# Splitting the modulation row of an adaLN block: scale first, values from unshifted rows, the shift added to the kv matrix afterwards

## The chip, the cores and the metric

The kernel runs on one core of one Trainium2 chip. The metric is the device time of one execution in microseconds (us), and the figure quoted for a kernel is the median of its fast runs unless something else is said. A profile is one execution seen by the hardware profiler; its span is about 2 us shorter than the device time of that execution. PE is the matmul engine, DVE the vector engine, ACT the scalar engine, POOL the GpSimd engine; SP issues most loads. "L764" is a line of the kernel. The line numbers differ between kernels, so the text says what each line does.

## The reference, cut to what matters

```python
mod = (silu(c) @ w_mod).reshape(1, 6, 1, -1)
sa, ca, ga, sb, cb, gb = (mod[:, i] for i in range(6))   # shift, scale, gate; twice
h = layernorm(x) * (1 + ca) + sa
q, k, v = split(h @ wqkv)                                # 2048 tokens, 32 heads of 32
pq, pk = phi(q), phi(k)                                  # elu + 1
kv = einsum('bhsd,bhse->bhde', pk, v);  z = pk.sum(tokens)
x = x + ga * ((pq @ kv) / (pq . z)) @ wo
h = layernorm(x) * (1 + cb) + sb
x = x + gb * (gelu(h @ w_gate) * (h @ w_up)) @ w_down    # the longest part of the time
```

Tokens are handled in four blocks of 512. A block has four x tiles of 128 tokens.

## The kernel before

A small planner records every operation, then orders each engine's instructions with a list scheduler that uses a model of costs. PE's order is the program's; the order on DVE, ACT, POOL and SP is the planner's. So one edit can move operations far away.

The opening loads two x tiles, then all 4 MB of the first modulation weights (`ModSet(0)` makes the shift row and the scale row together), then two more x tiles:

```python
def start_phase():
    xs = [load_x(0), load_x(1)]
    ms0 = ModSet(0, wm0_ring, psM)          # 8 loads of 512 KB: shift and scale
    xs += [load_x(2), load_x(3)]
    load_w(Wk[:, :, 0:NW], D, NW)
    ...
    xh = [ln_rows(x) for x in xs[0:2]]      # layernorm of rows on DVE
    transpose_h(halves[0], 0, xh[0]); keep_warm(3, NW)
    transpose_h(halves[0], 1, xh[1]); keep_warm(2, NW)
    for kt in range(KD):                    # row sums, with idle filler matmuls between
        ms0.step(); keep_warm(2, NW)
    ms0.columns(...)                        # row -> per-partition columns
    evac_h(0, halves[0])                    # h = xhat * scale + shift, from PSUM
    return [ln_rows(x) for x in xs[2:4]], halves[1]
```

`evac_h` evicts half of block 0: four operations on DVE, four on ACT. The second half follows after two key groups. Keys of block 0 come next (8 groups of 8 matmuls), then its values by a Strassen scheme (7 products, 56 matmuls), whose combinations, sums and copies run on DVE and ACT:

```python
blocks = [k0 + V[0]]                        # block 0: keys, then values
...
def comb(ps, sb, i, row, col):              # DVE, reads PSUM
    tt_op(dst(i, row, col), v3(ps), v3(sb), ALU.add)
```

Blocks 1 to 3 are normalized from x, written to memory, read back by a transposing load, and then scaled and shifted on DVE:

```python
def ln1_block(b):
    for tl in range(TT):
        xt = load_x(b * TT + tl)
        mv = ln_stats(xt)                   # DVE statistics
        rstd = pool_rstd(mv)                # POOL
        ve.scalar_tensor_tensor(out=nb, in0=mv[:, 0:1], scalar=-1.0, in1=rstd, ...)
        ac.activation(out=xh, in_=xt, func=AF.Identity, scale=rstd, bias=nb)
        gp.dma_start(out=xa_scr[b][...], in_=xh)
    sy.dma_start_transpose(out=hr1[b], in_=xa_scr[b][:])
    for kd in range(KD):
        ve.tensor_scalar(out=hr1[b][:, kd, :], ..., op0=ALU.mult, op1=ALU.add)
```

## Time and profile before

| | before |
|---|---|
| median of the first 5 runs | 778.31 us (777.8 to 781.81) |
| span of the profile | 776.5 us |
| PE busy | 754.3 us, 97% |
| first key matmul | 21.03 us |
| block 1's first key matmul | 54.48 us |
| block 2's first kv product | 85.68 us |

The page's first part gives the busy time of each engine, its share of the span and its number of instructions:

```profile
span 776.5 us, 10117 instructions
PE 754.3 (97%) x3656; PEld 345.3 (44%) x3680; DVE 553.2 (71%) x1091; ACT 376.7 (49%) x655; POOL 67.7 (9%) x142
```

PE is the bound of the whole, but a busy PE is not a useful PE. The timeline of PE (start, duration, engine, line, operation, shapes, count, and in brackets the idle time before it with what ended it) shows the opening. L489 makes row sums, L542 is filler, L764 keys, L557 transposes, L702 values:

```profile
16.65 0.40 PE L489 MATMUL psum<-mem 128*32 128x512 bf16 x4 [0.34 <-DMA mem<-in_w_mod_dram]
...
21.03 3.61 PE L764 MATMUL psum<-mem 128*128 128x512 bf16 x15 [2.04 <-DMA mem<-in_A_wqkv_dram]
24.48 1.06 PE L557 MATMUL psum<-mem 128*128 128x128 f16 x16
29.34 12.45 PE L764 MATMUL psum<-mem 128*128 128x512 bf16 x47 [3.80 <-DVE mem L549]
...
54.48 3.62 PE L764 MATMUL psum<-mem 128*128 128x512 bf16 x16
```

PE waits for the last modulation weights until 16.65 us, starts useful work at 21.03 us, and stands still for 3.80 us before 29.34 us. Then 47 matmuls take 12.45 us. Windows of 2 us (bounds, length, busy time of each engine with its count, then granted clock, DMA share and GB/s) show why they are slow, and three longer windows show DVE's load in the first 14 us, from there to block 1, and through block 1:

```profile
30.00:32.00 2.00, 2.00 (x6) 0.65 (x6) 1.90 (x5) 1.24 (x1) 1.15 (x3) 0.52 1.05 380
32.00:34.00 2.00, 2.00 (x7) 0.80 (x6) 1.97 (x7) 1.28 (x3) 0.21 (x1) 0.62 0.95 371
0.00:14.00 14.00, 7.52 (x51) 3.36 (x52) 5.15 (x22) 2.38 (x6) 2.64 (x20) 1.00 0.83 315
14.00:54.48 40.48, 33.27 (x165) 14.31 (x165) 34.63 (x86) 25.47 (x43) 10.66 (x21) 0.96 0.73 246
54.48:85.68 31.20, 31.04 (x167) 15.12 (x168) 22.55 (x58) 16.80 (x29) 5.06 (x9) 1.00 0.49 155
```

The clock was 0.52 and 0.62 of full speed after the standstill. DVE (the third busy time) worked 34.63 us of the 40.48 us between 14 us and block 1, but only 22.55 us of 31.20 in block 1.

### The profile page before, as it was taken

To read this page: it belongs to the slowest core of one execution; us is meant where nothing else is said; L and a number is where in the kernel's file an instruction comes from. 1 tells how busy PE (TensorE), PEld (TensorE's weight loads), DVE (VectorE), ACT (ScalarE), POOL (GpSimd) and SP (SyncE) were. 2 spreads that over 40 slices of the span, in tenths; PEclk is the share of its full clock that TensorE was granted. 3 is DMA by queue.
4 is the path that set the end of the run, shared out by engine and by line. 5 is a ranking of instruction groups with operands and counts; after the bars stand their busy time and mean duration, and the time that the engine had idled before them with its cause. 6 is when DMAs were issued, how large, how long until landed. Compare 5 with 4: busy or idle time off the path is not lost.

```text
span 776.5 us, 10117 instructions
## 1 busy us (share of the span) xinstructions
PE 754.3 (97%) x3656; PEld 345.3 (44%) x3680; DVE 553.2 (71%) x1091; ACT 376.7 (49%) x655; POOL 67.7 (9%) x142
## 2 busy tenths in 40 slices
PE   6799999999989999999999999999999999999997
PEld 2344545444434444444444444444444444444444
DVE  3895976479997877899878462776777767646254
ACT  1765656569779477775544202315455444430000
POOL 1230300000021212221000000010000000000000
PEclk9999999999999999999999999999999999999999
DMA  8837130591279747767566557852332323355441
GB/s 331 305 109 230 60 51 1 195 330 60 68 221 277 234 156 240 230 201 230 166 214 228 193 217 210 251 163 56 107 95 69 109 60 103 117 196 198 168 158 46
DMA packets 130178, 129.12 MB, mean 166 GB/s; under 512 B 32720, under 2 KB 109136, under 8 KB 129104
## 3 DMA queue, kind: packets, MB, share of 16 engines
q1 hardware_dynamic: 121600, 105.40, 43.7%
q0 software_dynamic: 6176, 20.98, 7.3%
q10 hardware_dynamic: 2352, 2.10, 0.8%
q8 instruction: 29, 0.48, 0.2%
q14 instruction: 21, 0.17, 0.1%
HBM read 98.04 MB, written 23.07 MB: 156 GB/s over the span
## 4 chain that ended last, share of the span: by engine, by line
PE 84%; DVE 6%; DMA 4%; ACT 3%; issue 1%; SPq 1%; POOL 0%; DVEq 0%; POOLq 0%; ACTq 0%
PE psum L1038 39%; PE psum L1143 22%; PE psum L764 7%; PE psum L702 5%; PE psum L945 5%; PE psum L730 4%; DVE mem L472 4%; DMA mem<-in_A_x_dram 1%; DVE mem L514 1%; DMA mem<-in_B_w_up_dram 1%; DMA mem<-in_w_mod_dram 1%; PE psum L775 1%; DMA mem<-in_B_w_down_dram 1%; DVE mem L800 1%; SPq L481 1%
## 5 line engine op out<-in xcount | busy, mean ns | idle before, releaser
L1038 PE MATMUL psum<-mem 128*128 128x512 f16 x1568 | 339.2, 379 | 0.3 <-ACT mem L633 0.2
L472 DVE TENSOR_TENSOR mem<-psum,mem 128x512 f16<-128x512 f32 (+3 forms) x302 | 202.1, 681 | 117.4 <-PE psum L1143 39.3
L1038 PEld LDWEIGHTS <-mem 128*128 128x128 f16 (+1 forms) x1568 | 153.4, 98 | 185.8 <-issue 1.1
L472 DVE TENSOR_TENSOR mem<-mem 128x1024 f16<-128x1024 bf16 (+9 forms) x415 | 211.5, 538 | 30.0 <-DMA mem<-in_B_w_up_dram 7.7
L633 ACT ACTIVATE mem<-psum 128x512 f32<-128x512 f32 x232 | 135.7, 594 | 178.2 <-PE psum L1038 89.2
L1143 PE MATMUL psum<-mem 128*128 128x512 f16 (+2 forms) x789 | 169.1, 375 | 0.5
L1143 PEld LDWEIGHTS <-mem 128*128 128x128 f16 x798 | 78.1, 98 | 91.4
L1051 ACT ACTIVATE mem<-mem 128x512 f16<-128x512 f16 x84 | 52.8, 629 | 77.7 <-DVE mem L472 77.7
L764 PE MATMUL psum<-mem 128*128 128x512 bf16 x244 | 59.5, 387 | 6.4 <-DVE mem L549 3.8
L945 PE MATMUL psum<-mem 128*128 128x512 f16 x256 | 57.9, 379 | 0.1
L730 PE MATMUL psum<-mem 128*128 128x512 f16 x224 | 51.2, 379 | 0.0
L702 PE MATMUL psum<-mem 128*128 128x512 f16 (+1 forms) x223 | 50.6, 379 | 0.7 <-ACT mem L633 0.6
L764 PEld LDWEIGHTS <-mem 128*128 128x128 f16 x256 | 25.2, 99 | 37.0 <-DVE mem L549 5.4
L945 PEld LDWEIGHTS <-mem 128*128 128x128 bf16 x256 | 24.8, 98 | 32.4 <-DVE mem L472 3.0
L621 ACT ACTIVATE mem<-psum 128x512 f16<-128x512 f32 x40 | 23.6, 594 | 27.8 <-PE psum L764 22.9
L730 PEld LDWEIGHTS <-mem 128*128 128x128 f16 (+1 forms) x224 | 21.4, 98 | 26.5 <-issue 2.1
L514 DVE BATCH_NORM_STATS2 mem<-mem 128x6 f32<-128x512 bf16 x48 | 31.7, 681 | 2.1 <-DMA mem<-in_A_x_dram 1.8
L702 PEld LDWEIGHTS <-mem 128*128 128x128 f16 x224 | 21.6, 98 | 25.8 <-issue 0.9
L626 DVE TENSOR_SCALAR mem<-mem 128x512 f16<-128x512 f16 x56 | 15.7, 284 | 15.7 <-ACT mem L621 15.5
L924 ACT ACTIVATE mem<-mem 128x512 f16<-128x512 f16 x28 | 20.3, 799 | 10.6 <-DMA mem<-xhs 10.6
L623 ACT ACTIVATE mem<-psum 128x512 f16<-128x512 f32 x40 | 23.7, 595 | 0.0
L788 ACT ACTIVATE mem<-psum,mem 128x512 f32<-128x512 f32 x32 | 21.4, 679 | 4.3 <-PE psum L786 3.3
(97 smaller groups left out, 383.0 us busy)
## 6 DMA issues: line engine op xcount, KB each, us to landing
mem<-in_B_w_gate_dram SPq DMA_DIRECT2D x28, 512.0 KB, 4.1
mem<-in_B_w_up_dram SPq DMA_DIRECT2D x28, 512.0 KB, 5.3
mem<-ts SPq DMA_DIRECT2D x8, 1792.0 KB, 6.9
mem<-in_w_mod_dram SPq DMA_DIRECT2D x24, 512.0 KB, 6.5
mem<-in_B_w_down_dram SPq DMA_DIRECT2D x6, 1792.0 KB, 7.5
mem<-in_A_x_dram SPq DMA_DIRECT2D x32, 256.0 KB, 3.9
mem<-in_B_w_down_dram SPq DMA_DIRECT2D x14, 512.0 KB, 6.0
ts<-mem POOLq DMA_DIRECT2D x14, 512.0 KB, 3.5
```

Source lines behind the costliest of these rows:

```text
L472: ve.tensor_tensor(out=out, in0=a, in1=b, op=op)
L514: ve.bn_stats(out=stats[:, cb, :], in_=xt[:, cb * BW:(cb + 1) * BW])
L621: ac.activation(out=e, in_=t, func=AF.Exp)
L623: ac.activation(out=r, in_=t, func=AF.Relu)
L633: ac.activation(out=t, in_=ps, func=AF.Copy)
L702: te.matmul(ps, lhsT=A[:, k, i * P:(i + 1) * P], rhs=B[:, k, :], start=(start and k == 0), stop=(k == KH - 1), skip_group_check=True)
L730: te.matmul(o, lhsT=W[:, k, (j0 + i) * P:(j0 + i + 1) * P], rhs=h_form(a, k), start=(start and k == 0), stop=(k == KH - 1), skip_group_che ...
L764: te.matmul(ps, lhsT=hr1[b][:, k, tl * P:(tl + 1) * P], rhs=Wk[:, k, n * NW:(n + 1) * NW], start=(k == 0), stop=(k == KD - 1))
L945: te.matmul(psw, lhsT=pqT[b][:, g, tl * P:(tl + 1) * P], rhs=Wp[:, g, cs], start=(g == 0), stop=(g == KD - 1))
L1038: te.matmul(ps, lhsT=a[:, u, k, :], rhs=b[:, k, :], start=(start and k == 0), stop=(k == KH - 1), skip_group_check=True)
L1051: ac.activation(out=t, in_=src, func=AF.Gelu_apprx_tanh)
L1143: te.matmul(ps, lhsT=a[:, i, q * P:(q + 1) * P], rhs=b[:, i, :], start=(start and i == 0), stop=(i == NPR - 1), skip_group_check=True)
```

## The change

The intent is to start useful matmuls with half of the modulation weights. Write block 0's rows as h = s + sa, where s = xhat * (1 + ca) needs only the scale. Then v = s Wv + sa Wv, and the kv matrix of the block is pk' (s Wv) + z (sa Wv). So the kernel can make block 0's values from s, and add z times one row, sa Wv, to the kv matrix later. Keys pass through a nonlinear phi and still need the full h. The core of the diff, with cuts:

```diff
 def start_phase():
-    xs = [load_x(0), load_x(1)]
-    ms0 = ModSet(0, wm0_ring, psM)
-    xs += [load_x(2), load_x(3)]
+    for tt in range(TT): xs.append(load_x(tt)); loads.append(plan.ops[-1])
+    ca = ModRow(1, wm_ca, {4: loads[2], 6: loads[3]})      # scale: 2 MB
+    load_w(Wv...)                                          # value weights, in three parts
+    sa = ModRow(0, wm_sa)                                  # shift: 2 MB
     load_w(Wk[:, :, 0:NW], D, NW)
 ...
+    for i in range(KH):
+        ca.step(i)
+        if i >= 0 and i < 2: tile_of(2 + i)                # transposes of tiles 2 and 3
+        keep_warm(2, NW)
+    ca.columns(opcA, 1.0, lambda: keep_warm(2, NW))
+    for f in scale: f()                                    # 32 small evictions: s = xhat * scale
+    for n, tl in ((0,0),(0,1),(0,2),(0,3),(1,0),(1,1)): v_plain(tl, n)   # 8 matmuls each
+    for i in range(KH): sa.step(i)
+    sa.columns(modT[:, 0:KD], 0.0, lambda: v_plain(2, 1))
+    v_plain(3, 1)
+    for kd in range(KD):                                   # h = s + shift, for the keys
+        ve.tensor_scalar_add(out=hr1[0][:, kd, :], in0=hs0[:, kd, :], scalar1=modT[:, kd:kd + 1])
+
+def shift_row():                                           # 16 narrow row sums: sa Wv
+    ...
+    def add(ch):                                           # during block 1
+        te.matmul(psr, lhsT=selr[:, ch, :], rhs=row, start=True, stop=True)
+        for g in range(4):                                 # kv += z * (sa Wv)
+            ve.scalar_tensor_tensor(out=o, in0=psr[...], scalar=kvzacc[:, 4*ch+g, P:P+1], in1=o, ...)
 ...
-blocks = [k0 + V[0]]
+blocks = [k0]                                              # block 0: only keys are left here
-    put(0, 2 + i, F(h_sum, 0, j), WV(j, 0), WV(j, 1))
-    put(1, i, F(h_sum, 1, j))
+    put(0, 3 + j, WV(j, 0), WV(j, 1))
+    put(1, i, F(h_sum, 0, j), F(h_sum, 1, j))              # block 0's sums move into block 1
 ...
+plan.moves = [(mods[1], kfin[3]), ([rows[3, 3]], relu)]    # two corrections to the planner's order
```

Left out above: the list of block 0 is now shorter, and the normalizing of blocks 1 and 2 is put at its steps 0 and 4 instead of 2 and 8.

The new `moves` take operations out of the planner's order and put them behind another operation. The first brings forward the scaling of block 1's rows on DVE. The second puts off the last normalized row of block 3 on ACT.

More of the change, by code (lines that the diff above doesn't have):

```diff
@@ L234, in order, with moved @@
         return [self.ops[n] for _, n in best[1]]
+    moves, drops, extra = (), (), ()
+    def moved(self):
+        ops = self.order()
+        for group, after in self.moves:
+            ops = [o for o in ops if o not in group]
+            i = ops.index(after) + 1
+            at = {o: j for j, o in enumerate(ops)}
+            late = [self.ops[p] for o in group for p in o.preds if self.ops[p] not in group and at[self.ops[p]] >= i]
+            assert not late, [(l.eng, l.line, at[l] - i) for l in late]
+            ops[i:i] = group
+        for group, before in self.extra:
+            i = ops.index(before)
+            ops[i:i] = group
+        return [o for o in ops if o not in self.drops]
     def issue(self):
         with self.tc.manual_schedule():
-            for op in self.order():
+            for op in self.moved():
                 if op.line not in self.calls:
@@ L326, with __init__ @@
     class Banks:
-        def __init__(self, lo, hi):
-            self.lo, self.n, self.i = lo, hi - lo + 1, 0
+        def __init__(self, lo, hi, skip=0):
+            self.lo, self.n, self.i = lo, hi - lo + 1, skip
         def __call__(self, dt=FP32):
@@ L352 @@
         nc.gpsimd.memset(selb[DH * j:DH * j + 1, j, :], 1.0)
+    sel2 = at(3.25, [2], F16)
+    nc.vector.memset(sel2, 0.0)
+    selr = at(164, [2, P], F16)
+    nc.gpsimd.memset(selr, 0.0)
+    for j in range(4):
+        nc.vector.memset(sel2[DH * j:DH * j + 1, j % 2:j % 2 + 1], 1.0)
+        nc.gpsimd.memset(selr[DH * j:DH * j + 1, j % 2, :], 1.0)
+    sarep = at(164.5, [KD, DH], F16)
     eps5 = at(1.75, [1], FP32)
@@ L378 @@
     vta = Ring(51.75, [KD, P + 2], F16, 4).slots
-    wm0_ring = Ring(60, [MW], BF16, 7)
-    wm0_ring.slots += Ring(176, [MW], BF16, 1).slots
+    wm_ca, wm_sa = at(60, [KD, D], BF16), at(176, [KD, D], BF16)
+    hs0 = at(152, [KD, TG], F16)
     Wq = at(60, [KD, D], BF16)
@@ L440 @@
     psK0, psK = Banks(4, 7), Banks(4, 5)
-    psD = Banks(5, 5)
+    psD, psV0, psR = Banks(5, 5), Banks(0, 5, 4), Banks(7, 7)
     QA, QB = Banks(0, 1), Banks(2, 3)
@@ L466, in load_x, with load_w @@
         return xt
-    def load_w(dst, col, n=D):
-        sy.dma_start(out=dst, in_=A_wqkv[:, col:col + n].rearrange("(kd p) n -> p kd n", p=P))
+    def load_w(dst, col, n=D, k0=0, k1=KD):
+        sy.dma_start(out=dst, in_=A_wqkv[k0 * P:k1 * P, col:col + n].rearrange("(kd p) n -> p kd n", p=P))
     def tt_op(out, a, b, op):
@@ L509, in spread, with __init__, step, columns @@
                 ac.activation(out=dst[:, h * NW:(h + 1) * NW], in_=psr, func=AF.Copy, scale=scale)
+    class ModRow:
+        def __init__(self, m, wm, before={}):
+            self.wm, self.ps = wm, None
+            for i in range(0, KD, 2):
+                sy.dma_start(out=wm[:, i:i + 2, :],
+                             in_=w_mod[i * P:(i + 2) * P, m * D:(m + 1) * D].rearrange("(k p) n -> p k n", p=P))
+                if i in before:
+                    plan.aim(before[i])
+        def step(self, i):
+            if i == 0:
+                self.ps = psM()
+            row_sums(self.ps, srep, self.wm, i)
+        def columns(self, dst, add, between=None):
+            row = mrow_ring()
+            ve.tensor_copy(out=row, in_=self.ps)
+            if between is not None:
+                between()
+            psc = psM()[:, 0:KD].rearrange("p (j c) -> p j c", c=2)
+            for jj in range(4):
+                te.matmul(psc[:, jj, :], lhsT=row[:, jj * P:(jj + 1) * P], rhs=sel2,
+                          start=True, stop=True, skip_group_check=True)
+            ve.tensor_scalar_add(out=dst.rearrange("p (c j) -> p c j", j=4), in0=psc.rearrange("p j c -> p c j"),
+                                 scalar1=add)
+    def row_sums(ps, rep, W, i):
+        for p in range(2):
+            for ch in range(2):
+                o = DH * (2 * p + ch)
+                te.matmul(ps[o:o + DH, :], lhsT=rep[:, 2 * i + p, :], rhs=W[:, 2 * i + p, ch * NW:(ch + 1) * NW],
+                          start=(i == 0), stop=(i == KH - 1))
     def ln_stats(xt):
@@ L543, in keep_warm, with start_tile, scale, v_plain @@
                              start=True, stop=True, skip_group_check=True)
-    def evac_h(h, pss):
-        for kd in range(KD):
-            src, dst = pss[kd // 4][:, kd % 4, :], hr1[0][:, kd, h * HB:(h + 1) * HB]
-            if kd < KD // 2:
-                ve.tensor_scalar(out=dst, in0=src, scalar1=opcA[:, kd:kd + 1], scalar2=modT[:, kd:kd + 1],
-                                        op0=ALU.mult, op1=ALU.add)
-            else:
-                ac.activation(out=dst, in_=src, func=AF.Identity, scale=opcA[:, kd:kd + 1],
-                                     bias=modT[:, kd:kd + 1])
-    def transpose_h(pss, tl, xh):
+    def start_tile(pss, tl, xh):
         for kd in range(KD):
             te.transpose(pss[kd // 4][:, kd % 4, (tl % 2) * P:(tl % 2 + 1) * P], xh[:, kd * P:(kd + 1) * P],
-                                ident)
-    def start_phase():
-        xs = [load_x(0), load_x(1)]
-        ms0 = ModSet(0, wm0_ring, psM)
-        xs += [load_x(2), load_x(3)]
+                         ident)
+        def scale():
+            for kd in range(KD):
+                src, dst = pss[kd // 4][:, kd % 4, (tl % 2) * P:(tl % 2 + 1) * P], hs0[:, kd, tl * P:(tl + 1) * P]
+                if kd < KH:
+                    ve.tensor_scalar_mul(out=dst, in0=src, scalar1=opcA[:, kd:kd + 1])
+                else:
+                    ac.activation(out=dst, in_=src, func=AF.Copy, scale=opcA[:, kd:kd + 1])
+        return scale
+    def v_plain(tl, n):
+        ps = psV0()
+        for k in range(KD):
+            te.matmul(ps, lhsT=hs0[:, k, tl * P:(tl + 1) * P], rhs=Wv[:, k, n * NW:(n + 1) * NW],
+                      start=(k == 0), stop=(k == KD - 1), skip_group_check=True)
+        ac.activation(out=vta[tl][:, 4 * n:4 * n + 4, 0:P], in_=ps.rearrange("p (g e) -> p g e", e=P), func=AF.Copy)
+    def start_phase():
+        xs, loads = [], []
+        for tt in range(TT):
+            xs.append(load_x(tt))
+            loads.append(plan.ops[-1])
+        ca = ModRow(1, wm_ca, {4: loads[2], 6: loads[3]})
+        load_w(Wv[:, 0:KH, 0:NW], 2 * D, NW, 0, KH)
+        load_w(Wv[:, KH:KD, 0:NW], 2 * D, NW, KH, KD)
+        load_w(Wv[:, :, NW:D], 2 * D + NW, NW)
+        sa = ModRow(0, wm_sa)
         load_w(Wk[:, :, 0:NW], D, NW)
@@ L574, in start_phase, with tile_of @@
         halves = [[psT(F16).rearrange("p (k t) -> p k t", k=4) for _ in range(2)] for _ in range(2)]
-        xh = [ln_rows(x) for x in xs[0:2]]
-        transpose_h(halves[0], 0, xh[0])
-        keep_warm(3, NW)
-        transpose_h(halves[0], 1, xh[1])
-        keep_warm(2, NW)
-        for kt in range(KD):
-            ms0.step()
-            if kt + 1 < KD:
-                keep_warm(2, NW)
-        ms0.columns(lambda: keep_warm(2, NW))
-        keep_warm(4, NW)
-        ve.tensor_scalar_add(out=opcA, in0=modT[:, KD:2 * KD], scalar1=1.0)
-        evac_h(0, halves[0])
-        return [ln_rows(x) for x in xs[2:4]], halves[1]
+        xh = [ln_rows(x) for x in xs]
+        scale = [None] * TT
+        def tile_of(tl):
+            scale[tl] = start_tile(halves[tl // 2], tl, xh[tl])
+        tile_of(0)
+        keep_warm(2, NW)
+        tile_of(1)
+        for i in range(KH):
+            ca.step(i)
+            if i >= 0 and i < 2:
+                tile_of(2 + i)
+            keep_warm(2, NW)
+        ca.columns(opcA, 1.0, lambda: keep_warm(2, NW))
+        for f in scale:
+            f()
+        for n, tl in ((0, 0), (0, 1), (0, 2), (0, 3), (1, 0), (1, 1)):
+            v_plain(tl, n)
+        for i in range(KH):
+            sa.step(i)
+        sa.columns(modT[:, 0:KD], 0.0, lambda: v_plain(2, 1))
+        v_plain(3, 1)
+        for kd in range(KD):
+            ve.tensor_scalar_add(out=hr1[0][:, kd, :], in0=hs0[:, kd, :], scalar1=modT[:, kd:kd + 1])
+    def shift_row():
+        ve.tensor_copy(out=sarep, in_=modT[:, 0:KD, None].to_broadcast((P, KD, DH)))
+        ps, row = psR(), mrow_ring()
+        for i in range(KH):
+            row_sums(ps, sarep, Wv, i)
+        ac.activation(out=row, in_=ps, func=AF.Copy)
+        def add(ch):
+            psr = psR()
+            te.matmul(psr, lhsT=selr[:, ch, :], rhs=row, start=True, stop=True)
+            for g in range(4):
+                o = kvzacc[:, 4 * ch + g, 0:P]
+                ve.scalar_tensor_tensor(out=o, in0=psr[:, g * P:(g + 1) * P],
+                                        scalar=kvzacc[:, 4 * ch + g, P:P + 1], in1=o, op0=ALU.mult, op1=ALU.add)
+        return [lambda ch=ch: add(ch) for ch in range(2)]
     def ln1_block(b):
@@ L598, in ln1_block @@
             ac.activation(out=xh, in_=xt, func=AF.Identity, scale=rstd, bias=nb)
+            rows[b, tl] = plan.ops[-1]
             gp.dma_start(out=xa_scr[b][tl * P:(tl + 1) * P, :], in_=xh)
@@ L603, in ln1_block @@
                              scalar2=modT[:, kd:kd + 1], op0=ALU.mult, op1=ALU.add)
+        mods[b] = plan.ops[-KD:]
     def h_sum(b, j):
@@ L610, in h_sum @@
                 (s4, a12, s2, ALU.subtract))[j])
+        hsums[b, j] = plan.ops[-1]
     def w_sum(W, WT, j, half):
@@ L755 @@
     NKB = (KD + GPB - 1) // GPB
-    pks = {}
+    rows, hsums, pks, kfin, kmm, mods = {}, {}, {}, [], [], {}
     def k_group(b, tl, n, mid=()):
@@ L765, in k_group @@
                              rhs=Wk[:, k, n * NW:(n + 1) * NW], start=(k == 0), stop=(k == KD - 1))
+        kmm.append(plan.ops[-KD:])
         for f in mid:
@@ L768, in k_group @@
         phi(pks[b, tl][:, n * NW:(n + 1) * NW], ps)()
+        kfin.append(plan.ops[-1])
     def kv_products(b, kb):
@@ L815, in kvq_phase @@
     def kvq_phase():
-        xh_b, pss_b = start_phase()
-        load_w(Wk[:, :, NW:D], D + NW, NW)
-        load_w(Wv, 2 * D)
         for t in vta:
             gp.memset(t[:, :, P:P + 1], 1.0)
-        def half_b():
-            transpose_h(pss_b, 2, xh_b[0])
-            transpose_h(pss_b, 3, xh_b[1])
-            evac_h(1, pss_b)
+        start_phase()
+        load_w(Wk[:, :, NW:D], D + NW, NW)
         def K(b, tl, n):
@@ L839, in F @@
             return lambda: f(*a)
-        V = {b: [S(f) for f in v_stages(b)] for b in range(NG)}
+        V = {b: [S(f) for f in v_stages(b)] for b in range(1, NG)}
         Q = {(pr, j): [S(f) for f in q_stages(pr, j)] for pr in range(2) for j in (0, 2)}
         k0 = [K(0, tl, n) for n in range(2) for tl in range(TT)]
-        blocks = [k0 + V[0]]
+        blocks = [k0]
         kk = [[K(b, tl, n) for tl in (2, 3, 0, 1) for n in (0, 1)] for b in range(NG)]
@@ L856, in kvq_phase @@
         WV, WQ = (lambda j, h: F(w_sum, Wv, WvT, j, h)), (lambda j, h: F(w_sum, Wq, WqT, j, h))
-        for b, at_b, at_i in ((1, 0, 2), (2, 0, 8), (3, 1, 4)):
+        for b, at_b, at_i in ((1, 0, 0), (2, 0, 4), (3, 1, 4)):
             put(at_b, at_i, F(ln1_block, b))
+        add_r = []
+        put(0, 1, lambda: add_r.extend(shift_row()))
+        put(1, 6, lambda: add_r[0]())
+        put(1, 8, lambda: add_r[1]())
         for j, i in enumerate((0, 1, 6, 6)):
-            put(0, 2 + i, F(h_sum, 0, j), WV(j, 0), WV(j, 1))
-            put(1, i, F(h_sum, 1, j))
+            put(0, 3 + j, WV(j, 0), WV(j, 1))
+            put(1, i, F(h_sum, 0, j), F(h_sum, 1, j))
             put(2, i, F(h_sum, 2, j), WQ(j, 0), WQ(j, 1))
@@ L869, in kvq_phase @@
             for i, step in enumerate(blocks[b]):
-                if (b, i) == (0, 2):
-                    half_b()
                 step(fill[b].get(i, ()))
@@ L1241 @@
         down_out(g)
+    at = plan.ops.index(kfin[16])
+    relu = [o for o in plan.ops[:at] if o.kw.get("func") == AF.Relu][-1]
+    plan.moves = [(mods[1], kfin[3]), ([rows[3, 3]], relu)]
     plan.issue()
```

## The prediction

> **What bounds the kernel now.** TensorE: 754.3 us busy of 776.5 (the page's first part); the chain of waits is 84% PE. So only PE idle time, slow-clock time and useless PE work can be won, and most is in the opening. The timeline: the first modulation rows need all 4 MB of their weights, for which PE waits until 16.65 us; the first useful matmul (keys) starts at 21.03 us; a gap of 3.80 us ends at 29.34 us, because x tiles 2 and 3 were queued behind the weights; then the granted clock is 0.52 and 0.62 (windows of 30 to 34 us, about 1.7 us lost). Keys and values of token block 0 (120 matmuls, 25.9 us at the later spacing of 216 ns) end at 54.48 us. DMA is at its limit until 32 us (350 to 420 GB/s); DVE is 9.0 to 9.6 of 10 us busy from 20 to 60 us.
>
> **What the change does.** It loads block 0's x first, then only the scale columns (2 MB), then value weights, then the shift. Block 0's values start from scaled, unshifted rows; the missing shift row is added later to the kv matrix, weighted by z. Added on PE: values by 64 plain matmuls for 56 (+1.7 us), 16 narrow row sums (about 1.1 us, as 16 others take 1.05 us), 2 spreads (0.4 us). On DVE: 8 shift additions (0.29 us each), 8 fix-ups (about 0.3 us each, estimate); removed: block 0's value combinations (0.6 to 0.7 us each). Its block sums move into block 1. PE's order after block 1's start hardly changes, so the gain must be made before and then kept.
>
> **Estimate of the new opening.** About 3.15 MB precede the end of the scale load: at the traced rates 11.0 us[...]. DVE's order puts the statistics of the next x tile (1.3 us, loaded behind the scale) before the copy of the scale row, so values start near 16 to 17 us, paced by scaling (16 small operations each on DVE and ACT, about 0.39 us each on ACT); their sixth group ends near 28 us. The shift's weights (8.4 MB in all) land near 26 us. Keys start near 31 to 32 us; block 0 ends near 47 us, against 54.48 us. Block 1's normalized rows (transposing load, then 8 DVE operations, 2.66 us) should be ready near 45 us, so they hardly block.
>
> Gain 7.5 us at block 1; I take off 0.5 us, as block 1 gets about 5 us more DVE work where it had some 8 us of slack. Later blocks shift as a whole. **Predicted 771 us, range 765.5 to 776; faster by over 2% 0.04, within 2% 0.94, slower by over 2% 0.02.**
>
> **What would show it.** Timeline: first value matmul at 15 to 18 us; no PE gap over 2.5 us before block 1; no window with a clock near 0.5 after 25 us. [...] Block 1's first keys at 45 to 49 us. From block 2 on, PE groups earlier by 6 to 9 us, constant to the end.
>
> **What would make it wrong.** DVE or ACT, saturated before 60 us, delays block 1's rows or key features, and the gain falls to 3 us or less; block 1's transposing load comes late behind 12 MB of queued loads; or, the other way, scale columns at 14 us, giving 10 us. The rescheduling could change a later wait by a few us.

Two passages are cut from it, where marked: a sentence on the clock that no run here shows, and a term for the landing of the scale load that no trace shows. With that term the way to the end of the scale load came to 12.5 us, on which the start of values at 16 to 17 us rests; that step was the author's estimate. The forecast's own sum: 778.31 us of before, less 7.5 us, plus 0.5 us, is 771 us. Measured figures to set beside it: in before the DMA share was 1.05 at 383 GB/s from 8 to 32 us, and DVE was busy for 9.05, 8.64, 9.64 and 9.40 us in the four windows of 10 us from 20 to 60 us; in the changed kernel a scaling took 0.41 us on ACT (median of 16), a shift addition 0.35 us (8 of them 2.2 us of DVE together) and a fix-up 0.34 us (8 of them 2.3 us together).

## More of the kernel before

The chain of waits (start, duration, what) has a piece that the prediction read too quickly:

```profile
6.64 7.93 DMA mem<-in_w_mod_dram
14.57 10.10 DMA mem<-in_A_x_dram
24.69 1.30 DVE mem L514 x2
29.34 6.19 PE psum L764 x19
```

The standstill is traced back to an x load issued at 14.57 us and to statistics (L514) at 24.69 us. DVE's timeline shows whose they are: three pairs of statistics of block 1's tiles stand in DVE's queue before the evictions (L549) of block 0. Its first line shows something else: until 17.10 us DVE stood idle for 8.39 us.

```profile
17.10 0.69 DVE L495 CAST mem<-psum 128x512 f16<-128x512 f32 x1 [8.39 <-PE psum L489]
...
24.69 1.29 DVE L514 BATCH_NORM_STATS2 mem<-mem 128x6 f32<-128x512 bf16 x2
...
26.14 1.23 DVE L514 BATCH_NORM_STATS2 mem<-mem 128x6 f32<-128x512 bf16 x2
...
27.53 1.23 DVE L514 BATCH_NORM_STATS2 mem<-mem 128x6 f32<-128x512 bf16 x2
28.80 0.21 DVE L516 BATCH_NORM_AGGREGATE mem<-mem 128x2 f32<-128x12 f32 x1
28.92 1.00 DVE L549 TENSOR_SCALAR mem<-psum,mem 128x256 f16<-128x256 f16 x3
```

## The result, and the profile after

The changed kernel takes 774.24 us median (773.21 to 776.04, 9 runs) against 779.11 us for before (16 runs of the same rounds): the ratio is 0.9935, with a 95% interval of 0.9924 to 0.9947. Ratios in this document are the mean time of one kernel's fast runs over that of the other's of the same rounds, so they are not quite the ratio of the medians quoted. The gain is 4.9 us by the medians, where 7.3 us were predicted.

```profile
span 772.2 us, 10183 instructions
PE 753.9 (98%) x3672; PEld 345.8 (45%) x3697; DVE 554.8 (72%) x1116; ACT 376.1 (49%) x664; POOL 67.1 (9%) x147
```

PE's timeline after, with plain values L624, row sums L568, keys L870 and kv products L883:

```profile
16.00 10.53 PE L624 MATMUL psum<-mem 128*128 128x512 bf16 x47 [0.58 <-DVE mem L615]
...
27.49 0.40 PE L568 MATMUL psum<-mem 128*32 128x512 bf16 x4 [0.20 <-DMA mem<-in_w_mod_dram]
...
31.39 3.62 PE L870 MATMUL psum<-mem 128*128 128x512 bf16 x16
...
50.20 0.87 PE L883 MATMUL psum<-mem 128*128 128x129 f16 x12 [0.30 <-ACT mem L729]
...
53.27 1.89 PE L870 MATMUL psum<-mem 128*128 128x512 bf16 x8 [0.47 <-ACT mem L729]
...
58.43 0.62 PE L883 MATMUL psum<-mem 128*128 128x129 f16 x8 [0.64 <-DVE mem L888]
...
80.05 0.86 PE L883 MATMUL psum<-mem 128*128 128x129 f16 x12
```

Values start at 16.00 us, the shift's weights come at 27.49 us, keys start at 31.39 us, and nothing stands still for 1 us from there to block 1. The first kv product of block 1 is at 50.20 us against 57.93 us before: 7.7 us ahead. Block 2's first kv product is at 80.05 us against 85.68 us: 5.6 us ahead. So 2.1 us were lost inside block 1, between these two marks, with the second and third of the waits shown and two new spread matmuls. (The first wait, 0.30 us, ends at the first mark.)

DVE's load in the first 14 us, from there to block 1, and in block 1 (third busy time), to be set beside the three long windows of before:

```profile
0.00:14.00 14.00, 6.92 (x57) 3.68 (x57) 10.21 (x37) 3.48 (x10) 3.86 (x25) 1.00 0.87 301
14.00:46.50 32.50, 31.46 (x176) 13.93 (x178) 27.91 (x83) 22.01 (x43) 10.04 (x20) 1.00 0.97 308
46.50:80.05 33.55, 31.86 (x167) 15.17 (x170) 29.06 (x79) 21.34 (x35) 9.05 (x18) 1.00 0.54 173
```

Between 14 us and block 1 DVE's work fell from 34.63 to 27.91 us, by 6.7 us. Most of this was not put off but done earlier: before 14 us DVE's work rose from 5.15 to 10.21 us, by 5.1 us, because all four x tiles are now loaded ahead of the weights, so that DVE makes the rows of tiles 2 and 3 and the first statistics of block 1 where it stood idle before. The remaining 1.7 us are the net of work taken out (value combinations, block sums), work added (such as the shift additions) and work that slipped past the start of block 1. In block 1 DVE's work rose from 22.55 to 29.06 us, by 6.5 us. From the start to block 2's first kv product DVE now works 67.17 us, against 62.34 us. The change did not take work off DVE; it added 4.8 us, but took 6.7 us out of the stretch where DVE was full.

From block 2 to the output projection the lead is constant (5.6 us). In this profile it falls to 4.6 us in the projection. There PE waits 0.89 and 1.24 us within 3 us, as it does in before, but here the clock fell after them. The same two windows of the same kernel in a second profile, `after_again` below, kept full clock, and there the lead was 5.0 us at block 2 and at the projection's end:

```profile
212.00:214.00 2.00, 1.33 (x4) 0.51 (x4) 1.97 (x6) 1.97 (x5) 0.59 (x2) 0.62 0.67 177
214.00:216.00 2.00, 2.00 (x7) 0.69 (x6) 1.41 (x5) 1.94 (x6) 0.30 (x1) 0.53 0.60 216
```

```profile
212.00:214.00 2.00, 0.76 (x5) 0.31 (x4) 2.00 (x5) 1.97 (x5) 1.08 (x2) 1.00 0.42 141
214.00:216.00 2.00, 1.86 (x8) 0.58 (x7) 1.97 (x7) 1.97 (x6) 0.00 (x0) 1.00 0.83 262
```

That loss, about 1 us, therefore does not belong to the change in every run.

**A fault in the changed kernel.** The second `move` takes the ACT operation that makes block 3's last normalized row and puts it behind a later one, but it leaves the write of that row where it was. In program order the write now comes first. The POOL line and the ACT line of the changed kernel's trace show it: the last of the twelve writes is issued at 78.14 us, the row is made at 80.60 us.

```profile
78.14 0.63 POOL L703 DMA_DIRECT2D xas<-mem  x1
```

```profile
80.60 1.24 ACT L701 ACTIVATE mem<-mem 128x1024 f16<-128x1024 bf16 x1 [1.00 <-DVE mem L497]
```

The write therefore stores what the buffer held before, the rows of block 2's last tile. It is no race (the order is fixed), and the comparison with the reference passes: putting those rows in place of the right 128 in the reference itself moves its output by 0.0014 in relative norm and at most 0.001 in value, because the attention branch is gated by small numbers. It is a wrong program all the same. The run `a_pair` moves the pair together; its time is that of the changed kernel.

### The profile page after: what moved, and what is told of

It reads as the page before. It is cut to its first block, busy times and chain, and to the rows that moved or that the text cites. A ratio compares the mean times of both kernels' runs of the same rounds, so it can differ in the third digit from the quotient of the medians.

```text
span 772.2 us, 10183 instructions
## 1 busy us (share of the span) xinstructions
PE 753.9 (98%) x3672; PEld 345.8 (45%) x3697; DVE 554.8 (72%) x1116; ACT 376.1 (49%) x664; POOL 67.1 (9%) x147
## 4 chain that ended last, share of the span: by engine, by line
PE 81%; DVE 9%; ACT 5%; DMA 3%; issue 2%; POOL 1%; SPq 0%; DVEq 0%; POOLq 0%
PE psum L1142 38%; PE psum L1247 22%; PE psum L1049 6%; PE psum L808 4%; PE psum L870 4%; PE psum L836 4%; DVE mem L497 4%; DVE mem L574 2%; DMA mem<-in_A_x_dram 2%; ACT mem L739 1%; PE psum L883 1%; DMA mem<-in_B_w_up_dram 1%; ACT mem L727 1%; ACT mem L729 1%; DVE mem L908 1%
## 5 line engine op out<-in xcount | busy, mean ns | idle before, releaser
L497 DVE TENSOR_TENSOR mem<-psum,mem 128x512 f16<-128x512 f32 (+4 forms) x296 | 197.2, 680 | 119.9 <-PE psum L1247 40.4
L739 ACT ACTIVATE mem<-psum 128x512 f32<-128x512 f32 x226 | 132.0, 594 | 175.6 <-PE psum L1142 89.8
L1247 PEld LDWEIGHTS <-mem 128*128 128x128 f16 x798 | 78.1, 98 | 91.4
L870 PE MATMUL psum<-mem 128*128 128x512 bf16 x244 | 57.2, 379 | 1.2 <-ACT mem L729 0.5
L870 PEld LDWEIGHTS <-mem 128*128 128x128 f16 x256 | 24.9, 98 | 30.3 <-issue 1.2
L808 PE MATMUL psum<-mem 128*128 128x512 f16 (+1 forms) x168 | 38.4, 379 | 0.0
L727 ACT ACTIVATE mem<-psum 128x512 f16<-128x512 f32 x40 | 23.6, 593 | 19.7 <-PE psum L870 19.7
L808 PEld LDWEIGHTS <-mem 128*128 128x128 f16 x168 | 16.2, 98 | 18.4
L729 ACT ACTIVATE mem<-psum 128x512 f16<-128x512 f32 x40 | 23.8, 598 | 0.0
```

The source lines that it names most:

```text
L497: ve.tensor_tensor(out=out, in0=a, in1=b, op=op)
L727: ac.activation(out=e, in_=t, func=AF.Exp)
L729: ac.activation(out=r, in_=t, func=AF.Relu)
L739: ac.activation(out=t, in_=ps, func=AF.Copy)
L808: te.matmul(ps, lhsT=A[:, k, i * P:(i + 1) * P], rhs=B[:, k, :], start=(start and k == 0), stop=(k == KH - 1), skip_group_check=True)
L870: te.matmul(ps, lhsT=hr1[b][:, k, tl * P:(tl + 1) * P], rhs=Wk[:, k, n * NW:(n + 1) * NW], start=(k == 0), stop=(k == KD - 1))
```

## The experiments

All gave a result that passes the comparison. Each is timed over 5 rounds against before on the same chip. The planner re-plans after any edit, so the milestones below matter more than the totals. They were read from PE's timelines (us):

| run | block 0's keys start | block 1's first kv product | block 2's first kv product | keys start to there | projection | FFN start | span |
|---|---|---|---|---|---|---|---|
| before | 21.03 | 57.93 | 85.68 | | 200.46 | 263.97 | 776.5 |
| b_warmgap | 20.50 | 56.92 | 84.94 | | 199.71 | 264.70 | 776.6 |
| b_evac | 20.83 | 58.47 | 86.22 | | 200.99 | 264.50 | 777.1 |
| b_evacm | 20.27 | 62.41 | 90.15 | | 204.92 | 268.43 | 780.4 |
| after | 31.39 | 50.20 | 80.05 | 48.66 | 194.82 | 259.35 | 772.2 |
| after_again | 32.26 | 50.88 | 80.72 | 48.46 | 195.48 | 258.99 | 771.0 |
| a_pair | 32.21 | 51.00 | 80.84 | 48.63 | 195.59 | 259.09 | 771.8 |
| a_nokw | 32.66 | 51.12 | 80.96 | 48.30 | 195.71 | 260.40 | 773.0 |
| a_rows2 | 32.54 | 50.89 | 80.54 | 48.00 | 195.29 | 258.79 | 772.1 |
| a_rows23 | 33.05 | 51.40 | 80.25 | 47.20 | 195.01 | 258.51 | 771.5 |
| a_best | 32.62 | 50.97 | 79.91 | 47.29 | 194.68 | 258.19 | 770.5 |
| a_hsum2 | 33.98 | 52.32 | 81.58 | 47.60 | 196.34 | 263.35 | 775.2 |
| a_nofix | 32.78 | 50.05 | 78.93 | 46.15 | 193.70 | 259.15 | 771.6 |

The start of the keys varies between 31.39 and 33.05 us for nearly the same opening. In the changed kernel it follows the landing of the shift's weights, which ended PE's wait at 27.49 us in one profile and at 28.21 us in the other. The column "keys start to there" takes this out in part, but it also shrinks a little when keys start later (48.66, 48.46 and 48.30 us in after, after_again and a_nokw). The cleanest measure of the loss in block 1 is the distance between the two kv products: 27.75 us in before; 29.85, 29.84, 29.84 and 29.84 us in after, after_again, a_pair and a_nokw; 29.65 us in a_rows2, 28.85 in a_rows23, 28.94 in a_best, 29.26 in a_hsum2 and 28.88 in a_nofix.

Two theories stood against each other. **Order:** PE's waits in block 1 come from the order of work on ACT and DVE, where ready work for PE stands behind an operation that itself waits (for 3.11 us on ACT, below). **Load:** DVE simply has too much to do in block 1 (29.06 us of 33.55). For the gain there were also two: removing PE's standstill and slow clock, or relieving DVE before block 1.

### a_pair: the fault repaired

```diff
-plan.moves = [(mods[1], kfin[3]), ([rows[3, 3]], relu)]
+row = lambda b, tl: [plan.ops[rows[b, tl].n + d] for d in (0, 1)]     # the row and its write
+plan.moves = [(mods[1], kfin[3]), (row(3, 3), relu)]
```

> The changed kernel with the last normalized row of token block 3 moved together with its write to memory (in the kernel as given, only the ACT operation is moved, and its trace shows the write at 78.14 us, before the operation that makes the row, 80.60 us). Theory: only a correctness repair, the write is some 3.5 us later, and block 3's transposing load has slack until block 3 starts near 117 us. Expect the same time as the changed kernel, 0.9935 of the kernel before, within 0.1%. Rival: the early write was part of the gain; then 0.5 to 3 us are lost again.

Measured: 773.82 us, ratio 0.9939 (0.9925 to 0.9953). The write is now issued at 81.81 us, after its row at 80.28 us. The gain did not rest on the fault.

### a_rows2 and a_rows23: order on ACT and DVE in block 1

ACT's timeline of the changed kernel shows what PE's first two waits in block 1 stood behind (L727 and L729 are exp and relu of keys, L701 normalizes rows of a later block):

```profile
44.20 0.62 ACT L729 ACTIVATE mem<-psum 128x512 f16<-128x512 f32 x1
47.94 1.24 ACT L701 ACTIVATE mem<-mem 128x1024 f16<-128x1024 bf16 x1 [3.11 <-DVE mem L699]
```

ACT stood idle for 3.11 us at the head of its queue, for statistics of a row of block 2, while keys were ready. The row itself is next used by block 2's transposing load, issued at 54.98 us, 7 us later. ACT did not pass the waiting row in this trace: the exp of the ready keys ran right after it, at 49.09 us.

```diff
+of = lambda i: plan.ops[kfin[i].n - 2]                # relu of the i-th key group
 plan.moves = [(mods[1], kfin[3]), (row(3, 3), relu),
+              (row(2, 2), of(7)), (row(2, 3), of(8)),                               # a_rows2
+              ([plan.ops[rows[3, 0].n - 1]] + row(3, 0), of(10))]                   # a_rows23
```

> As a_pair, and block 2's normalized rows 2 and 3 (ACT, with their writes) are moved behind the key features of block 0's last group and block 1's first group. Theory, ACT's in-order queue: the 3.11 us that ACT waits at 47.94 us for block 2's row statistics holds back exp and relu of keys that are ready; so PE's waits at 50.20 us (0.30) and 53.27 us (0.47) vanish and PE runs 0.7 to 1.0 us earlier from block 2 on: ratio about 0.9925. Rival, DVE is simply overloaded in block 1 (5 us of work added): the wait only moves to the key additions on DVE, and the time stays at a_pair's within 0.2 us.

Measured for a_rows2: 773.92 us, ratio 0.9937 (0.9923 to 0.9950), no gain by time. Both waits on ACT are gone, but a new one stands behind them, on DVE:

```profile
55.72 0.85 PE L886 MATMUL psum<-mem 128*128 128x129 f16 x12 [0.52 <-DVE mem L891]
```

Keys to block 2 take 48.00 us against 48.63 in a_pair. The wait near 50 us is no proof: after_again and a_nokw do not show it either, without this edit. The one near 53 us, 0.47 us in all four profiles without the edit, is gone by it, and 0.52 us stand one queue further; between the two kv products only 0.2 us are gained. The theory was right about the second wait and wrong about what it was worth.

> As a_rows2, and block 3's first row (its DVE bias operation, its ACT operation, its write) is moved behind block 1's third key group. Theory: this removes the PE wait at 58.43 us (0.64 us), where the copy of the first kv products waits on DVE behind that bias operation, which waits 1.00 us for POOL; ratio about 0.9915, PE 1.4 to 1.9 us ahead of the changed kernel from block 2 on. Rival, DVE overload: no gain over a_pair.

Measured for a_rows23: 773.3 us, ratio 0.9930 (0.9914 to 0.9947). Keys to block 2 take 47.20 us, 1.4 us less than a_pair, with about the same work on DVE. Between the two kv products, where the 2.1 us were lost, it is 1.0 us less (28.85 against 29.84 us): so much of the loss is order. What stays there is the two spreads (0.4 us) and a wait on DVE, shown as 0.51 us. The time alone does not resolve it: the interval overlaps a_pair's.

### a_best: one more wait, and the changed kernel again

PE waited 0.51 us in a_rows23 for a copy of kv products that stood behind a block sum and statistics on DVE. a_best puts these behind the copy:

```diff
+              ([hsums[1, 3]], kvc[0]), ([plan.ops[rows[3, 0].n - d] for d in (6, 5, 4)], kvc[0])]
```

> As a_rows23, and on DVE one block sum and the statistics of block 3's first tile come after the first copy of kv products, which PE waited for in that run (0.51 us at 56.23 us). Theory: that wait goes too, and from key start to block 2's first kv product it takes 46.7 us (47.20 in a_rows23, 48.66 in the changed kernel): ratio near 0.992, 1.0 to 1.9 us under the changed kernel. Rival: the wait moves to the next operation in the queue again.

> The changed kernel again, for comparison on the same chip: ratio 0.9935 within 0.1%. Its profile shows whether the slow clock near 213 us in the first one (0.62 and 0.53 after two waits of 0.89 and 1.24 us) belongs to the kernel[...]: a_pair has the same waits and kept full clock there.

Measured: a_best 772.73 us, ratio 0.9915 (0.9901 to 0.9929); the changed kernel in the same rounds 773.79 us, ratio 0.9933 (0.9918 to 0.9948). Here the rival was right: the wait at 56.23 us is gone, a wait of 0.60 us stands at 58.30 us, and keys to block 2 take 47.29 us, as in a_rows23 and not the 46.7 us expected. a_best has the lowest time of all runs, is a repaired program, and has no useless step more than the changed kernel; but its two intervals overlap, so its lead over the changed kernel, some 1.1 us by the medians, is likely and not proved.

### a_hsum2 and a_nofix: load on DVE in block 1

```diff
-put(1, i, F(h_sum, 0, j), F(h_sum, 1, j))
-put(2, i, F(h_sum, 2, j), WQ...)
+put(1, i, F(h_sum, 1, j))
+put(2, i, F(h_sum, 0, j), F(h_sum, 2, j), WQ...)     # a_hsum2: 2.7 us of DVE to block 2
```

> The changed kernel with block 0's four sums of its halves (2.7 us of DVE) moved from block 1 to block 2. Rival, DVE overload in block 1: PE gains 0.5 us or more by block 2, counted from the landing of the shift's weights, though block 2 may lose it again. Theory, order on ACT and DVE and not load: PE waits at 50.2, 53.3 and 58.4 us stay within 0.2 us, and so does the time.

Measured: 776.22 us, ratio 0.9965 (0.9951 to 0.9978), slower than the changed kernel. In block 1 it did help: keys to block 2 take 47.60 us, 1.1 us less than after, of which 0.6 us lie between the two kv products (where DVE's work fell only from 25.94 to 25.40 us, since other work moved in); the waits near 50 and 53 us are gone, while the one near 58 us stays. So the expectation of the order theory failed here: the block also became shorter without a further move by hand. But the planner also changed the opening (values start at 17.28 us, after a wait of 1.24 us for the scale row's copy, and 48 of their matmuls take 12.22 us, against 10.53 us in a_pair) and the projection, where the stretch to the FFN grew from 63.5 to 67.0 us with 2.9 us of new waits on DVE. The edit is confounded, and only the stretch in block 1 speaks to the question.

```diff
-put(0, 1, lambda: add_r.extend(shift_row()))          # a_nofix: no repair of the kv matrix
-put(1, 6, lambda: add_r[0]())
-put(1, 8, lambda: add_r[1]())
```

> The changed kernel without the shift row's repair: no row sums of the value weights, no spreads, no fix-ups of the kv matrix (a wrong result on purpose, perhaps too small for the comparison to see). Theory, its price is PE instructions alone: 1.05 us for 16 row sums and 0.43 us for two spreads, so PE is 1.5 us earlier at block 2, counted from the landing of the shift's weights; ratio about 0.9915. Rival, DVE overload: the eight fix-ups (about 2.3 us of DVE) are felt too, and the gain is 2.3 us or more.

Measured: 773.27 us, ratio 0.9929 (0.9913 to 0.9944). Its result is wrong on purpose, and the comparison passes it too. Keys to block 2 take 46.15 us, 2.5 us less than after (2.2 us less than a_nokw, whose keys start as late): 1.5 us of PE instructions, the rest less waiting. By time only 0.5 us or so is left, less than the intervals resolve, because the projection took 65.45 us against 63.50 us in a_pair, with 2.6 us of new waits on DVE that the new plan brought. The price of the algebraic repair is thus 2.2 to 2.5 us where it is paid.

Order and load are not exclusive. Of the 2.1 us, order alone gives back 1.0 us with about the same load; a_hsum2, in the planner's order, gives back 0.6 us, but with so little less load between the marks that it does not price load alone.

### a_nokw: is the opening bound by PE or by the shift's weights?

```diff
-            keep_warm(2, NW)                          # after each scale step
```

> The changed kernel without the two idle filler matmuls after each of the four scale steps. Theory: the scale row is PE-bound there (no wait for its weights is recorded), so value matmuls start up to 0.6 us earlier (the copy then waits for the statistics ending at 13.9 us); but keys need the shift row, whose weights land near 27.4 us, so PE waits that much longer there and block 0 ends as before: time equal to the changed kernel within 0.3 us, PE wait for the shift's weights up from 0.20 to about 0.8 us. Rival: PE order is what limits, and all after is 0.6 to 1 us earlier. Also, if the clock falls without the fillers, value matmuls run slower at first.

Measured: 774.52 us, ratio 0.9945 (0.9931 to 0.9960). Values start at 15.82 us, 0.2 us earlier; the wait for the shift's weights is 0.58 us, and the keys start at 32.66 us after another wait of 0.52 us on DVE. The value matmuls were not slower: 11 took 2.55 us and the other 37 took 8.17 us, where 47 took 10.53 us in after. The projection took 64.69 us against 63.50 us in a_pair, with the same waits of 0.89 and 1.24 us, and the mean clock of the profiled run was 0.998 against 1.000. In the first profile of the changed kernel, also at 0.998, it took 64.53 us, with the clock at 0.62 and 0.53 after these waits, and in the second 63.51 us; so the edit is probably not what made this profile's FFN start late. Nothing is gained by a faster start of values, so the fillers cost nothing here.

### b_xfirst: a run that did not test what it was made for

```diff
-    xs = [load_x(0), load_x(1)]
+    xs = [load_x(tt) for tt in range(TT)]
     ms0 = ModSet(0, wm0_ring, psM)
-    xs += [load_x(2), load_x(3)]
```

> The kernel before with one thing of the change: all four x tiles of block 0 are loaded ahead of the modulation weights; nothing is split or added. Theory A (most of the gain is the new order of loads): weights end 1.3 us later, so keys start near 22 us, but the 3.80 us gap before 29.34 us and the slow clock after it (1.7 us) go; block 0 ends near 51 us and the ratio is about 0.996, more than half of the change's gain. Theory B (the gain is the split of scale and shift, with values first): at most 1 us is gained, since keys still wait for all 4 MB of weights, and block 1's rows are not ready earlier; ratio 0.9985 or more.

Measured: 779.72 us, ratio 1.0008 (0.9994 to 1.0021). The planner did not keep the order: it put tile 2 behind six of the eight weight loads and tile 3 behind all. The first run of six, the profiled one, was slow (893.39 us at a clock of 0.849); it took no part in the ratio. Its order is still readable: tile 2's statistics began at 14.23 us against 17.71 us before, and PE still stood still for 3.15 us. Earlier x tiles did not shorten the gap much, but as a test of the full reordering the run is void: DVE worked 5.16 us in its first 14 us, as in before, and not the 10.21 us of the changed kernel. So theory A, that the new order of loads alone makes much of the gain, stays untested.

### b_warmgap: the price of the slow clock

```diff
             transpose_h(pss_b, 3, xh_b[1])
+            for _ in range(16):                       # idle fillers on a free PSUM bank
+                te.matmul(psm[:, 7, :], lhsT=ident, rhs=..., start=True, stop=True, ...)
```

> The kernel before with 16 idle filler matmuls (3.5 us) on a free PSUM bank in the 3.80 us gap after the second pair of transposes. Theory: the gap stays, but the clock does not fall to 0.52 and 0.62 after it: keys of block 0 run at full clock, PE is about 1.7 us ahead at block 1, ratio about 0.998. Rival: block 1's rows (last of them 55.5 us) hold PE back, so nothing is left by block 2.

Measured: 778.45 us, ratio 0.9991 (0.9978 to 1.0004), no clear gain. The clock stayed at 1.00 in both windows of 30 to 34 us, and the keys that took 12.45 us for 47 matmuls took 10.91 us for 48. Block 1 began 1.1 us earlier, block 2's first kv product came 0.7 us earlier, and the rest was lost in the projection, where this profile's clock fell to 0.55 and 0.59 after the two waits (0.89 and 1.24 us) that before has too, at full clock. So of the 1.7 us that the slow clock cost, 1 us was swallowed before and in block 1.

### b_evac and b_evacm: the standstill removed, without the change

```diff
+plan.moves = [(evac[5:9], evac[4])]                    # b_evac: DVE evictions right after the transposes
+plan.moves = [(evac[5:9], evac[4]), (mods[1], kfin[6])]   # b_evacm
```

> The kernel before with DVE's order changed in one place: the four evictions of block 0's second half come right after its transposes, ahead of 4.1 us of statistics for block 1 (24.69 to 28.80 us in the trace of before). Theory: the 3.80 us gap before 29.34 us was that order on DVE, not late x tiles; keys then restart near 26 to 27 us, the clock does not fall, and block 0's matmuls are 4 us ahead. By then block 1's rows (last scaled at 55.5 us on DVE, no earlier here) hold PE, so less than 2 us is left at block 2; ratio 0.998 to 1.0. Rival: the x tiles' landing is what counts, and the gap stays above 3 us.

Measured: 777.75 us, ratio 0.9980 (0.9968 to 0.9993). PE's timeline (L785 keys, L723 values, L654 copies on ACT, L489 combinations on DVE):

```profile
27.10 10.84 PE L785 MATMUL psum<-mem 128*128 128x512 bf16 x47 [0.28 <-DVE mem L568]
37.78 3.62 PE L723 MATMUL psum<-mem 128*128 128x512 bf16 x16
42.68 1.89 PE L723 MATMUL psum<-mem 128*128 128x512 f16 x8 [1.28 <-ACT mem L654]
45.77 1.02 PE L723 MATMUL psum<-mem 128*128 128x512 f16 x4 [1.20 <-DVE mem L489]
...
51.57 3.61 PE L723 MATMUL psum<-mem 128*128 128x512 f16 x15 [1.76 <-ACT mem L654]
55.02 3.62 PE L785 MATMUL psum<-mem 128*128 128x512 bf16 x16
```

The stretch from the end of the keys to block 1, by engine:

```profile
37.78:55.02 17.24, 12.77 (x57) 5.43 (x56) 16.86 (x41) 11.84 (x18) 5.45 (x10) 1.00 0.43 118
```

The standstill is 0.28 us instead of 3.80 us, and the keys ran at full clock (1.00 from 25 to 55 us) and ended at 37.78 us, 3.8 us ahead of before (41.62 us). Then the Strassen values waited for DVE and ACT, and block 1 started at 55.02 us, 0.5 us later than before. This is the run that tells the two theories of the gain apart. PE's standstill was real, it was made by DVE's order, and in this profile it was worth nothing: DVE, busy for 16.86 of the 17.24 us from the end of the keys to block 1, still had its 34.6 us of work to do. By time 1.5 us of the change's 4.9 were gained. Where, the profile does not show (the profiled run, 778.86 us, is the slowest of its six).

> As b_evac, and the eight operations that scale block 1's rows come right after the phi of block 0's seventh key group on DVE, as the change also moves them forward. Theory: block 1 can then start near 51 us; PE is 2 to 4 us ahead at block 2, ratio 0.995 to 0.9975, so a good part of the change's 4.9 us could be had by DVE's order alone, without splitting scale and shift. Rival: the rows are not landed by then (their transposing load), DVE waits, and nothing is gained; then the split's earlier block 1 rows are what counts.

Measured: 782.10 us, ratio 1.0039 (1.0026 to 1.0053), slower. The scaling of block 1's rows came earlier and pushed the value combinations back on a DVE that was full. The chain went through ACT to PE:

```profile
52.79 4.00 PE L723 MATMUL psum<-mem 128*128 128x512 f16 x9 [4.46 <-ACT mem L654]
```

PE stood still for 4.46 us, and the clock fell to 0.50 after it. Moving work within the full stretch gained nothing here; the change moves it out, most of it to before 14 us.

## Why the prediction was right or wrong

The measured time, 774.24 us, lies in the predicted range of 765.5 to 776 us, and the forecast "within 2%" holds. The predicted gain was 7.3 us, the measured one 4.9 us.

- **The opening was right.** Values started at 16.00 us (predicted 16 to 17), the sixth group ended near 26.5 us (28), the shift's weights came at 27.49 us and 28.21 us in the two profiles (26), keys started at 31.39 and 32.26 us (31 to 32). Block 1 was 7.7 and 7.1 us ahead (7.5) by its first kv product.
- **One step inside it was wrong.** The statistics of the next x tile were said to delay the copy of the scale row. They ran before it, but the copy then waited 0.47 us for PE: PE was the later of the two. The start of values, 16.00 us, thus came out right for another reason than the one given, which is luck.
- **The step that failed was mis-sized: "I take off 0.5 us, as block 1 gets about 5 us more DVE work where it had some 8 us of slack".** DVE's extra work was 6.5 us, the slack was 8.65 us (31.20 less 22.55), and the loss was 2.1 us in both profiles. Slack over a whole stretch is an average. Between the two marks PE waited 0.47 and 0.64 us (and 0.30 us just before the first) for single operations that stood in a queue behind something not yet ready, and the two spreads took 0.4 us. Order alone gave 1.0 us of this back (a_rows23).
- **"Later blocks shift as a whole" held up to the projection.** The lead was 5.6 and 5.0 us there, below the 6 to 9 us named. After that one profile lost another 1.0 us to a slow clock, so that the mark "no window with a clock near 0.5 after 25 us" failed in it, and the second profile did not. Runs of edited kernels lost up to 3.5 us there to new plans. The warning that rescheduling could change a later wait by a few us was right for the experiments, more than for the change.
- **The reading of before was wrong in one cause.** "Because x tiles 2 and 3 were queued behind the weights" does not explain the 3.80 us: their rows were normalized at 23.8 us and transposed by 25.5 us. DVE did 4.1 us of block 1's statistics first. The chain of waits had said so.
- **So the reason for the gain was only half right.** The prediction counted PE's idle and slow-clock time as the prize. b_evac took nearly all of that away and gained 1.5 us. What the change has beyond it is 6.7 us less DVE work between 14 us and block 1: 5.1 us are done before 14 us, because the x tiles come first, and 1.7 us net are taken out, where plain values need no combinations on DVE and the block sums went to block 1. Lower DVE work beside the earlier block is what the two profiles show; that it is the cause is supported by b_evac and b_evacm, where DVE's load stayed and block 1 did not come earlier, but not shown. A run with the split and the old load on DVE was not made, and b_xfirst did not test the x tiles alone; so the shares of the earlier values, of the earlier x tiles and of the work taken out stay open.

## What to carry to other kernels

When an idle stretch of the bounding engine lies next to a stretch where a second engine is full, ask when that second engine can be done: filling the gap alone may only move the wait a few microseconds on (in b_evac 3.5 us of standstill went and 1.5 us of time). Look for work that can leave the full stretch, first to an earlier time at which that engine is idle, then to a later one, even at the price of more matmuls. Count that engine's work from the very start: a window that begins at 14 us hid here that 5.1 us had only moved ahead of it. Then look in the receiving stretch for single operations that wait at the head of an engine's queue, since average slack does not protect against them (here 2.1 us were lost beside 8.65 us of slack). When an operation is moved by hand, move its consumers with it and check that order by the trace, because a comparison with a tolerance may not see 128 wrong rows.

## What the runs show of the clock and of waiting engines

- The clock fell to 0.62 and 0.53 after two waits of 0.89 and 1.24 us, 2.1 us in all, with one matmul recorded between them, in the first profile of the changed kernel, and stayed at 1.00 after the same waits in its second profile, after_again. It fell after the same two waits in b_warmgap too (0.55 and 0.59), and stayed at 1.00 in before, a_pair, a_rows23 and a_best. With the fall the projection took 64.53 and 64.99 us, without it 63.5 us. Of the other profiles with these waits, a_rows2, b_evac and b_evacm took 63.5 us for it, a_nokw 64.69 us. So a standstill as long as the 3.80 us of before, after which the clock was 0.52 and 0.62, was not needed for a fall. What decides it is not shown.
- One execution of b_xfirst, a program of one core, ran at a mean granted clock of 0.849 (0.85 from 36 us to the end; 0.50 in the windows of 30 to 34 us, after a standstill of 3.15 us) and took 893.39 us, where its other runs took 779 to 780 us. The cause is not shown.
- In the changed kernel ACT stood idle for 3.11 us with ready keys behind it, and PE's two waits behind it were 0.77 us together; of the 0.47 us that the edit surely removed (a_rows2), nearly all came back as a wait of 0.52 us on DVE.
